# Banded attention and a gated convolution FFN on one core: the planner counts TensorE's changes of array shape, and the work is divided anew

## The chip, the cores and the metric

The kernel runs on one core of one Trainium2 chip. The metric is the device time of one execution in microseconds (us). Five engines work beside each other: TensorE (PE in the profile, its weight loads PEld), VectorE (DVE), ScalarE (ACT), GpSimd (POOL) and SyncE (SP), which here issues nearly all DMAs.

## The reference, cut to what matters

```python
# q, k, v: (8 batches, 8 heads, 576 positions, 64), float32
scores = q @ k.T / 8                      # per batch and head
scores = where(abs(i - j) <= 32, scores, -1e9)
x = softmax(scores) @ v                   # heads joined: (8, 576, 512)
h = maximum(x @ w_in, 0)                  # w_in: 512 x 1024
conv = sum(conv_w[t] * h shifted by t - 1 along the sequence for t in 0, 1, 2)
out = (h * sigmoid(conv)) @ w_out         # w_out: 1024 x 512, out float32
```

## The kernel before, in words

**Attention.** The work of a batch is split by pairs of heads. `cast_qk` and `cast_q_turned` (POOL) make bfloat16 copies of q and k; `tr_mm` transposes them on TensorE into PSUM and `tr_copy` copies them out in two parts, one by ACT and one by DVE, cut at row `CUT` (`CUTH` for the first two batches) of nine. For the batches in `TURNED` a DMA transposes q. Because only a band of 32 positions to each side is needed, scores are computed for a 64-wide query tile against a 128-wide key window. `score` is a matmul with a contraction of 64, so it uses one half of TensorE's rows, and heads of a pair go to the two halves: `sch_mm`, `scl_mm` and `sc_mm` are the row-halves matmuls. ACT takes the exponential, DVE multiplies by the 0/1 band mask. `av_mm` and `avc_mm` multiply by v, with 64 output partitions each: these are the column-halves matmuls. A column of ones beside v gives the sums; DVE divides (`sum_rec`, `av_norm`, `avc_norm`). `castv` (POOL) makes the bfloat16 v, `shift_v` (keys `voc`; POOL, or DVE for batches below `VP`) a copy shifted by 64 rows. The result x is transposed on TensorE (`xt_mm`, first two batches) or by a DMA (`xt_dma`).

**FFN.** The 4608 rows of all batches are cut into 12 chunks of 384 (`c`), and d_ff into 8 blocks of 128 (`m`): 96 conv blocks. `ph_mm` computes a block of h (4 matmuls of some 385 columns), `relu` (ACT) writes it to hT with weight 0.5. The convolution of a block goes one of three ways (`conv_by`): on TensorE (`pc_mm`, 3 matmuls with diagonal weights made by `make_diag`), on ACT and DVE (`conv_acc`: one scaled copy by ACT into PSUM, two multiply-adds by DVE), or on POOL (`conv_pool`, five instructions). `tanh` (ACT) and `gate` (DVE) finish it, `py_mm` multiplies by w_out (8 matmuls of 512 columns for 128 rows), `y_copy` and `y_store` write out. Chunks 0 and 1 are worked in two halves of 192 columns. All FFN and transpose matmuls use the whole array.

**Order.** Each piece of work is entered with `add`: engine, a wished time `want`, a duration, what it depends on and which PSUM banks or buffers it takes and gives back. `Planner.run` is a list scheduler that runs when the program is built: it plays the durations through, picks for each engine among the pieces that could start soonest the one with the earliest `want`, and the pieces are emitted in that fixed order on every engine. Its durations therefore decide the order, not the time on the chip. Where the plan leaves TensorE idle in its first 30 us, `fill` puts in dummy matmuls. Wished times come from constants: `chunk_at(c)` is `S2 + (c - 2) * PC`, batches are placed ahead of their chunks (`want_of_b`), loads ahead of batches (`LEAD`, `LD`).

Of the kernel before, what the change touches and what calls it, by code (L numbers as in the profile page):

```python
# [16 lines left out]
class Op:  # L17
# [3 lines left out]
    def __init__(self, eng, want, dur, lat, fn, deps, takes, gives, dma, early, ring, shared):  # L21
        self.eng, self.want, self.dur, self.lat, self.fn, self.early = eng, want, dur, lat, fn, early
        self.ring, self.shared = ring, shared
        self.deps, self.takes, self.gives, self.dma = deps, takes, gives, dma


class Planner:

# [7 lines left out]
    def add(self, key, eng, want, dur, fn, deps=(), lat=None, takes=(), gives=(), dma=None,  # L36
            early=0.0, ring="SP", shared=False):
        if lat is None:
            lat = {"ACT": 0.16, "DVE": 0.14, "POOL": 0.08}.get(eng, 0.12)
        assert key not in self.ops, key  # L40
        self.ops[key] = Op(eng, want, dur, lat, fn, deps, takes, gives, dma, early, ring,
                           shared or eng == "POOL")

    def run(self, fill, until):
# [16 lines left out]
        order = []  # L61

# [31 lines left out]
        while done < len(ops):  # L94
            best = None
            for e, now in engines.items():
# [8 lines left out]
                if not starts:  # L105
# [22 lines left out]
            engines[e] = start + op.dur  # L128
            end = start + op.dur + op.lat
# [31 lines left out]
def kernel(  # L161
# [27 lines left out]
    BH = 2  # L189
# [118 lines left out]
    QK, V96, V128, WQ = 1.75, 0.9, 1.1, 1.7  # L308
# [277 lines left out]
    def ph_mm(c, m, part, ps):  # L586
        x0, x1 = cols_of(c, part)
        for kc in range(KC):
            x_ = xT_pp[c // 3 % 2][:, x0 // S, kc, x0 % S:x0 % S + min(x1 - x0, S - x0 % S)]
            if x0 < S < x1:  # L590
# [3 lines left out]
                pf[ps[0]][:, 0:x1 - x0], w_in_sb[:, kc, m * 128:(m + 1) * 128], x_,  # L594
# [3 lines left out]
    def relu(c, m, part, ps):  # L598
        kind = c % 3
# [3 lines left out]
        from_ = pf[ps[0]][:, 0:n]  # L603
        if kind == 1 and part is None:
            base = hT[:, m, 0:HW + 1]
            to = bass.AP(base.tensor, base.offset, [list(base.ap[0]), [HW + 3, 2], [1, HW + 1]])
            from_ = from_.rearrange("p (i x) -> p i x", i=2)
        elif kind == 1:
            to = hT[:, m, (HW + 3) * part:(HW + 3) * part + HW + 1]
        else:  # L610
            o0 = (1 if kind == 0 else 0) + x0 - cols_of(c, None)[0]
            to = hT[:, m, o0:o0 + n]
        if relu_by(c, m) == "ACT":
            scalar.activation(to, from_, AF.Relu, bias=0.0, scale=0.5)
        else:
            vector.tensor_scalar(
                out=to, in0=from_, scalar1=0.5, scalar2=0.0, op0=ALU.mult, op1=ALU.max
            )

    def taps(c, m, part, kk):  # L620
        kind = c % 3
        step = HW + (2 if kind == 1 else 0)
        base = hT_pp[kind][:, m, kk:kk + HW]
        return bass.AP(
            base.tensor, base.offset + step * (part or 0),
            [list(base.ap[0]), [step, 2 if part is None else 1], [1, HW]],
        )

    def pc_mm(c, m, part, ps):
        n = CH if part is None else HW  # L630
        for kk in range(3):
            tensor.matmul(
                pf[ps[0]][:, 0:n], diag_w[:, kk, m, :], taps(c, m, part, kk),
                start=(kk == 0), stop=(kk == 2),
            )

    def halves(t_):
        return t_[:, 0:CH].rearrange("p (i x) -> p i x", x=HW)

    def conv_pool(c, m, step, a, b):  # L640

        a, b = halves(ca_pp[a]), halves(cb_pp[b])
        if step in (0, 1, 3):
            kk = (step + 1) // 2
            pool.tensor_scalar(
                out=b if step else a, in0=taps(c, m, None, kk), scalar1=conv_w_sb[:, kk, m:m + 1],
                scalar2=None, op0=ALU.mult,
# [4 lines left out]
    def conv_acc(c, m, kk, ps):  # L652

        to, w_ = halves(pf[ps[0]]), conv_w_sb[:, kk, m:m + 1]
        if kk == 0:
            scalar.activation(to, taps(c, m, None, kk), AF.Copy, bias=0.0, scale=w_)
        else:
            vector.scalar_tensor_tensor(
                out=to, in0=taps(c, m, None, kk), scalar=w_, in1=to, op0=ALU.mult, op1=ALU.add
            )  # L660

    def tanh(c, m, part, ps, from_=None):
        n = CH if part is None else HW
        from_ = pf[ps[0]] if from_ is None else from_
        scalar.activation(pf[ps[0]][:, 0:n], from_[:, 0:n], AF.Tanh, bias=0.0, scale=1.0)

    def gate(c, m, part, ps):
        n = CH if part is None else HW
        o0 = HW * (part or 0)
        vector.scalar_tensor_tensor(  # L670
            out=gT_pp[c % 3][:, m, o0:o0 + n].rearrange("p (i x) -> p i x", x=HW),
            in0=pf[ps[0]][:, 0:n].rearrange("p (i x) -> p i x", x=HW), scalar=1.0,
            in1=taps(c, m, part, 1), op0=ALU.add, op1=ALU.mult,
        )
# [38 lines left out]
    TURNED = (4, 6, 7)  # L713
    XT_N = 2
    DTX = 1.22
    XQ_AT = 0.0
    QW = 1.6
    RELU_DVE = {}
    VP = 2
# [6 lines left out]
    MO, ME = 7.0, 9.0  # L726
    NACT = 3
    LD = 1.7
    PC = 14.2
    S2 = 55.0  # L730
# [12 lines left out]
    DIAG_T = 18.0  # L743
# [28 lines left out]
    for m in range(MB):  # L772
        for kk in range(3):
            engine = "DVE" if kk in DIAG_DVE else "ACT"
# [6 lines left out]
    def qk_loads(b, i):  # L781
# [4 lines left out]
        for y in range(2):  # L786
# [4 lines left out]
            else:  # L791
                got.append((("load", b, y, i), QK, lambda b=b, y=y, i=i: load_qk(b, y, i), after[y]))
# [56 lines left out]
    for b in range(B):  # L849
# [41 lines left out]
        if b < BH:  # L891
            sch = lambda bb: [("sch", bb, f, x, zs) for f in range(2) for x in range(NPH)
                              for zs in HALF_PAIRS[f]] if bb >= 0 else []
            for f in range(2):
# [17 lines left out]
                for i in range(NPH):  # L912
                    for zs in HALF_PAIRS[f]:
# [3 lines left out]
                        add(sk, "PE", ts, 2 * n * 0.021,  # L917
# [9 lines left out]
        for i in range(NPH if b >= BH else 0):  # L927
# [25 lines left out]
            add(lk, "PE", ts, 4 * 0.021, lambda ps, gi=gi: scl_mm(gi, ps), turned + before,  # L953
# [4 lines left out]
            for z in range(2):  # L958
# [3 lines left out]
                add(sk, "PE", ts, 16 * 0.021, lambda ps, g=g: sc_mm(g, ps),  # L962
# [22 lines left out]
        for c in range(NBLK):  # L985
            xdeps = [("ph", (b // 2 - 2) * 3 + z, m, part) for z in range(3) for m in range(MB)
                     for part in (None, 0, 1)]
            if cmajor:
                tx = HALF_AT[b][c > 1] + 4.0 + 0.9 * (c - 2 * (c > 1))
                ak = ("avc", b, c)  # L990
                add(ak, "PE", tx, 16 * 0.026, lambda ps, b=b, c=c: avc_mm(b, c, ps),
# [42 lines left out]
    def relu_by(c, m):  # L1034
        return "DVE" if m in RELU_DVE.get(c, ()) else "ACT"

# [12 lines left out]
    for c in range(NCH):  # L1049
        ps_ = parts.get(c, (None,))  # L1050
        for m in range(MB):
            for part in ps_:
                n = cols_of(c, part)[1] - cols_of(c, part)[0]
                w = CH if part is None else HW
                if c < 2:
                    t = FF_AT[c + part] + FF_STEP[c + part] * m + 0.6 * c * (1 - part)
                else:
                    t = chunk_at(c) + m * PC / (MB + 0.5)
                gap = (3.4 if c == NCH - 1 else 2.4) if part is None else 1.0
                hk, ck = ("ph", c, m, part), ("pc", c, m, part)  # L1060
                add(hk, "PE", t, KC * (n / 2400.0 + 0.003),
                    lambda ps, c=c, m=m, part=part: ph_mm(c, m, part, ps),
# [111 lines left out]
```

## Time and profile before

| | |
|---|---|
| median of 3 runs | 223.59 us (221.87, 223.59, 224.38) |
| profiled execution | 222.25 us, of which the span from first to last instruction is 220.4 us |
| TensorE clock granted | 1.000 |
| PE / DVE / ACT / POOL busy | 208.4 / 181.8 / 187.7 / 169.9 us |
| DMA | 48.28 MB, 219 GB/s over the span |

Busy time of an engine is the union of its instructions' times; idle time inside it is read from the rows' brackets, which name what ended it. The time outside the span, 1.85 us, is taken as it is. Nearly every instruction carries the number of one helper line (L251), so groups are told apart by the tiles they write and read, `out<-in`: `pf` is PSUM.

### The profile page before, as it was taken

To read this page: it belongs to the slowest core of one execution; us is meant where nothing else is said; L and a number is where in the kernel's file an instruction comes from. 1 tells how busy PE (TensorE), PEld (TensorE's weight loads), DVE (VectorE), ACT (ScalarE), POOL (GpSimd) and SP (SyncE) were. 2 spreads that over 40 slices of the span, in tenths; PEclk is the share of its full clock that TensorE was granted. 3 is DMA by queue.
4 is the path that set the end of the run, shared out by engine and by line. 5 is a ranking of instruction groups with operands and counts; after the bars stand their busy time and mean duration, and the time that the engine had idled before them with its cause. 6 is when DMAs were issued, how large, how long until landed. Compare 5 with 4: busy or idle time off the path is not lost.

```text
span 220.4 us, 6695 instructions
## 1 busy us (share of the span) xinstructions
PE 208.4 (95%) x2578; PEld 134.5 (61%) x2602; DVE 181.8 (83%) x361; ACT 187.7 (85%) x414; POOL 169.9 (77%) x204
## 2 busy tenths in 40 slices
PE   7898898999999988998999999999999999999993
PEld 7887797877666655554556555555565555545442
DVE  5388698997659999979898979969899989897930
ACT  3998698987797998699998898888999799999941
POOL 4663865787899999999799997789969449999600
PEclk9999999999999999999999999999999999999999
DMA  5999999996999999999999996999964325121123
GB/s 174 259 247 335 315 265 298 362 315 152 332 336 206 229 330 197 236 301 273 238 280 350 235 216 146 227 322 246 277 162 109 89 73 154 48 95 51 48 95 143
DMA packets 81667, 48.28 MB, mean 219 GB/s; under 512 B 64076, under 2 KB 69476, under 8 KB 81636
## 3 DMA queue, kind: packets, MB, share of 16 engines
q1 hardware_dynamic: 81600, 47.85, 85.4%
q8 instruction: 20, 0.33, 0.7%
q14 instruction: 11, 0.09, 0.1%
q10 hardware_dynamic: 36, 0.01, 0.0%
HBM read 32.52 MB, written 9.44 MB: 190 GB/s over the span
## 4 chain that ended last, share of the span: by engine, by line
PE 63%; DMA 11%; POOL 7%; ACT 6%; SPq 6%; DVE 4%; issue 3%; ACTq 0%; POOLq 0%
PE pf L251 63%; SPq L251 6%; DMA qT<-qb 4%; DMA vst<-in_v_dram 4%; POOL vo L251 3%; DMA wst<-in_moe_w_in_dram 3%; ACT pf L251 2%; ACT hT L251 2%; ACT attn L251 1%; POOL ve L251 1%; DVE attn L251 1%; DVE vo L251 1%; POOL w_in_sb L251 1%; ACT y L251 1%; DVE gT L251 1%
## 5 line engine op out<-in xcount | busy, mean ns | idle before, releaser
L251 PE MATMUL pf<-xT,w_in_sb 128*128 128x385 bf16 (+3 forms) x448 | 75.0, 305 | 2.6 <-POOL w_in_sb L251 0.8
L251 PE MATMUL pf<-w_out_sb,gT 128*128 128x512 bf16 (+1 forms) x272 | 66.1, 373 | 1.2
L251 DVE SCALAR_TENSOR_TENSOR gT<-pf,hT 128x384 bf16<-128x384 f32 (+1 forms) x112 | 52.7, 489 | 8.3 <-ACT pf L251 7.9
L251 PEld LDWEIGHTS <-w_in_sb 128*128 128x128 bf16 x448 | 40.5, 98 | 23.5 <-issue 2.0
L251 DVE SCALAR_TENSOR_TENSOR pf<-hT,conv_w_sb,pf 128x384 f32<-128x384 bf16 x86 | 51.6, 609 | 3.7 <-ACT pf L251 3.2
L251 ACT ACTIVATE hT<-pf 128x385 bf16<-128x385 f32 (+3 forms) x112 | 48.3, 462 | 3.7 <-PE pf L251 3.4
L251 ACT ACTIVATE pf<-pf 128x384 f32<-128x384 f32 (+1 forms) x102 | 43.6, 442 | 4.7 <-PE pf L251 3.2
L251 PEld LDWEIGHTS <-gT 128*128 128x128 bf16 x296 | 28.0, 98 | 28.7 <-issue 0.2
L251 ACT ACTIVATE attn<-pf 128x1024 bf16<-128x1024 f32 (+2 forms) x48 | 37.7, 816 | 0.4 <-PE pf L251 0.3
L251 POOL TENSOR_SCALAR vo<-ve 64x520 bf16<-64x520 bf16 x48 | 33.7, 702 | 3.7
L251 DVE TENSOR_TENSOR attn<-attn,mask 128x1152 bf16<-128x1152 bf16 (+2 forms) x32 | 29.3, 925 | 6.6 <-ACT attn L251 6.4
L251 ACT COPY y<-pf 128x512 f32<-128x512 f32 (+1 forms) x36 | 21.1, 585 | 13.0 <-PE pf L251 12.8
L251 POOL TENSOR_SCALAR ve<-vst 128x512 bf16<-128x512 f32 x40 | 26.6, 669 | 6.9 <-DMA vst<-in_v_dram 5.1
L251 PE MATMUL pf<-hT,diag_w 128*128 128x192 bf16 (+1 forms) x177 | 29.8, 283 | 0.2 <-ACT hT L251 0.2
L251 POOL TENSOR_SCALAR qb<-qst 128x512 bf16<-128x512 f32 (+1 forms) x22 | 19.7, 898 | 9.5 <-DMA qst<-in_q_dram 9.2
L251 DVE TENSOR_TENSOR xn<-pf,rec 128x640 bf16<-128x640 f32 (+1 forms) x34 | 26.3, 778 | 0.4
L251 ACT ACTIVATE pf<-hT,conv_w_sb 128x384 f32<-128x384 bf16 x43 | 25.5, 598 | 0.6 <-DVE xn L251 0.2
L251 POOL TENSOR_SCALAR cb<-hT,conv_w_sb 128x384 f32<-128x384 bf16 x20 | 25.1, 1259 | 0.2
L251 POOL TENSOR_SCALAR kb<-kst 128x1152 bf16<-128x1152 f32 x16 | 19.1, 1195 | 3.4 <-DMA kst<-in_k_dram 3.1
L251 POOL TENSOR_TENSOR ca<-ca,cb 128x384 f32<-128x384 f32 x20 | 20.2, 1019 | 0.5
L251 POOL TENSOR_SCALAR ca<-hT,conv_w_sb 128x384 f32<-128x384 bf16 x10 | 12.4, 1246 | 7.8 <-ACT hT L251 7.7
L251 PEld LDWEIGHTS <-diag_w 128*128 128x128 bf16 x177 | 14.6, 97 | 5.9 <-issue 0.6
(48 smaller groups left out, 227.9 us busy)
## 6 DMA issues: line engine op xcount, KB each, us to landing
out_dram<-y SPq DMA_DIRECT2D x35, 256.0 KB, 3.0
kst<-in_k_dram SPq DMA_DIRECT2D x12, 576.0 KB, 6.7
vst<-in_v_dram SPq DMA_DIRECT2D x24, 256.0 KB, 4.4
qst<-in_q_dram SPq DMA_DIRECT2D x6, 576.0 KB, 7.4
vst<-in_v_dram SPq DMA_DIRECT2D x16, 192.0 KB, 5.5
qst<-in_q_dram SPq DMA_DIRECT2D x6, 512.0 KB, 5.0
qst<-in_q_dram SPq DMA_DIRECT2D x8, 288.0 KB, 6.4
kst<-in_k_dram SPq DMA_DIRECT2D x8, 288.0 KB, 6.0
```

The source lines that it names most:

```text
L251: return lambda *args, **kwargs: fixed(do(*args, **kwargs))
```

## The change

The planner gives each piece of TensorE work a mode (0 whole array, 1 row halves, 2 column halves). A piece whose mode differs from that of the piece before starts 0.097 us later in the plan; after a halves piece, other halves pieces count as wished 3 us earlier. Planned durations of the halves matmuls are lowered, those of the first q and k loads raised (`QK0`). Nearly all constants of the order are set anew. In chunks 0 and 1 `relu`, `tanh` and `gate` take two blocks in one instruction (`PAIR_R`, `PAIR_G`; in chunk 10 `tanh` and `gate` only, where neither block is POOL's). Nine of the 24 diagonal weights are made by DVE. `shift_v` of batch 2 goes to DVE, half of batch 0's to POOL. `CUT` goes from 4 to 5 and `CUTH` from 3 to 2. One load of w_out goes ahead of the first loads of batch 1. POOL has the same blocks as before, but for m = 2 in the place of m = 0 in chunk 8. A block that stands in both lists is POOL's: the lists take 53 blocks off TensorE before and 57 after.

```diff
+    MODES = {"sch": 1, "scl": 1, "sc": 1, "av": 2, "avc": 2}
+    DRAIN = 0.097
...
+        def gain(op):
+            if op.eng != "PE" or not mode or not op.mode:
+                return 0.0
+            return same if op.mode == mode else other
...
-                    key=lambda k: (ops[k].want, number[k]),
+                    key=lambda k: (ops[k].want - gain(ops[k]), number[k]),
                 )
+                if e == "PE" and ops[key].mode != mode:
+                    starts[key] = max(starts[key], now + self.DRAIN)
...
+            if e == "PE":
+                mode = op.mode
...
-    QK, V96, V128, WQ = 1.75, 0.9, 1.1, 1.7
+    QK, V96, V128, WQ = 1.75, 0.9, 1.1, 1.75
+    QK0 = (((1.75, 2.6), (2.0, 1.85)), ((1.85, 1.85), (1.85, 1.85)))
...
-    CUT = 4
+    CUT = 5
-    W1, W2, W3 = 0, 0, 2
-    HALF_AT = ((4.0, 16.0), (24.0, 30.0))
-    FF_AT = (13.0, 24.0, 38.0)
-    FF_STEP = (1.2, 1.6, 1.2)
-    PY_AT = 4.0
-    LEAD = 18.0
-    VOC0 = ("DVE", "DVE")
-    DIAG_DVE = ()
+    W1, W2, W3 = 0, 1, 2
+    HALF_AT = ((4.0, 18.0), (24.0, 30.0))
+    FF_AT = (15.0, 24.0, 32.0)
+    FF_STEP = (1.2, 1.2, 0.8)
+    PY_AT = 0.0
+    LEAD = 6.0
+    VOC0 = ("POOL", "DVE")
+    DIAG_DVE = (0, 1, 2)
-    CUTH = 3
+    CUTH = 2
-    DTX = 1.22
-    XQ_AT = 0.0
+    DTX = 2.0
+    XQ_AT = -1.0
-    VP = 2
+    VP = 3
-    MO, ME = 7.0, 9.0
+    MO, ME = 7.0, 8.0
-    LD = 1.7
-    PC = 14.2
-    S2 = 55.0
+    LD = 1.0
+    PC = 11.0
+    S2 = 54.0
...
-            engine = "DVE" if kk in DIAG_DVE else "ACT"
+            engine = "DVE" if m in DIAG_DVE else "ACT"
...
-                        add(sk, "PE", ts, 2 * n * 0.021,
+                        add(sk, "PE", ts, 2 * n * 0.015 + 0.008,
-                    add(ak, "PE", ta, 20 * 0.024, lambda ps, g=g: av_mm(g, ps),
+                    add(ak, "PE", ta, 20 * 0.0165, lambda ps, g=g: av_mm(g, ps),
...
-    POOL_LAG = 8.0
-    ON_POOL = {2: (0,), 3: (), 4: (0,), 5: (0,), 6: (), 7: (0,), 8: (0,), 9: (0, 2), 10: (0, 2), 11: (0,)}
-    ON_DVE_2 = (1, 3, 4, 6)
-    ON_DVE_3 = (1, 3, 5, 6)
-    ON_DVE_4 = (1, 2, 3, 5, 6)
-    ON_DVE_5 = (1, 3, 5, 6)
-    ON_DVE_6 = (1, 3, 5, 6)
-    ON_DVE_7 = (1, 3, 4, 6)
-    ON_DVE_8 = (1, 3, 5, 6)
-    ON_DVE_9 = (1, 3, 4, 5, 6)
-    ON_DVE_10 = (1, 3, 4, 5, 6)
-    ON_DVE_11 = (1, 2, 4, 5)
+    POOL_LAG = 5.0
...
+    ON_DVE_2 = (0, 3, 5, 6)
+    ON_DVE_3 = (1, 2, 3, 5, 7)
+    ON_DVE_4 = (2, 3, 6, 7)
+    ON_DVE_5 = (0, 2, 5, 6, 7)
+    ON_DVE_6 = (0, 2, 4, 5, 6, 7)
+    ON_DVE_7 = (1, 2, 6, 7)
+    ON_DVE_8 = (0, 1, 3, 4, 5, 7)
+    ON_DVE_9 = (1, 3, 4, 5, 6, 7)
+    ON_DVE_10 = (1, 3, 4, 5, 6)
+    ON_DVE_11 = (0, 1, 2, 4, 5)
...
+    PAIR_R = (0, 1)
+    PAIR_G = (0, 1, 10)
...
-    plan.run(fill, 30.0)
+    SAME, OTHER = 3.0, 3.0
+    plan.run(fill, 30.0, SAME, OTHER)
```

More of the change, by code (lines that the diff above doesn't have):

```diff
@@ L952 @@
             lk = ("scl", gi)
[L953 removed]
+            add(lk, "PE", ts, 4 * 0.015 + 0.008, lambda ps, gi=gi: scl_mm(gi, ps), turned + before,
                 lat=PL, takes=[("p", 2)])
@@ L1032, in conv_by, with groups_of, gates, gates_of @@
         return "POOL" if m in ON_POOL.get(c, ()) else "DVE" if m in ON_DVE.get(c, ()) else "PE"
-    def relu_by(c, m):
-        return "DVE" if m in RELU_DVE.get(c, ()) else "ACT"
+    PAIR_R = (0, 1)
+    PAIR_G = (0, 1, 10)
+    def groups_of(c, conv):
+        got = []
+        for m in range(0, MB, 2):
+            if c in (PAIR_G if conv else PAIR_R) and not (
+                    conv and "POOL" in (conv_by(c, m), conv_by(c, m + 1))):
+                got.append((m, m + 1))
+            else:
+                got += [(m,), (m + 1,)]
+        return got
+    by_relu = {(c, m): ms for c in range(NCH) for ms in groups_of(c, False) for m in ms}
+    by_gate = {(c, m): ms for c in range(NCH) for ms in groups_of(c, True) for m in ms}
+    def gates(c):
+        return [("gate", c, m, p) for m in range(MB) for p in (None, 0, 1)]
+    def gates_of(c, m):
+        ms = by_gate.get((c, m), (m,))
+        return [("gate", c, ms[0], p) for p in (None, 0, 1)]
+    def relu_key(c, m, part):
+        return "relu", c, by_relu[c, m][0], part
     def xt_need(c, part):
```

261 lines of the change are left out of this document (153 added, 108 removed).

## The prediction

> **What bounds the kernel now.** I read the page's busy times first, then a table by stretches, then TensorE's timeline in the middle of the run.
>
> ```profile
> PE 208.4 (95%) x2578; PEld 134.5 (61%) x2602; DVE 181.8 (83%) x361; ACT 187.7 (85%) x414; POOL 169.9 (77%) x204
> ```
>
> The stretches (columns: PE, PEld, DVE, ACT, POOL busy, TensorE clock, DMA share, GB/s) are the start, the stretch of chunks 0 and 1 in half-size matmuls, the long middle with attention and FFN mixed, and the FFN-only end:
>
> ```profile
> 0.00:23.00 23.00, 19.29 (x343) 17.73 (x344) 14.05 (x39) 17.20 (x40) 12.78 (x20) 1.00 0.91 259
> 23.00:50.00 27.00, 25.76 (x431) 22.68 (x430) 23.90 (x57) 23.47 (x70) 18.97 (x24) 1.00 1.07 305
> 50.00:180.00 130.00, 126.63 (x1608) 74.56 (x1627) 114.79 (x211) 115.50 (x234) 110.79 (x137) 1.00 1.00 235
> 180.00:210.00 30.00, 29.64 (x174) 15.74 (x172) 27.30 (x53) 28.65 (x66) 27.38 (x25) 1.00 0.23 74
> ```
>
> From 23 to 210 us TensorE stands idle only 1.24 + 3.37 + 0.36 = 5.0 us, at full clock. DVE is busy 88% and ACT 89% of the middle, 91% and 96% of the end stretch. So TensorE sets the pace, and the two engines behind it have 4 to 12% in hand. Is that busy time work? The timeline of TensorE (start, length, work):
>
> ```profile
> 125.19 1.48 PE L251 MATMUL pf<-xT,w_in_sb 128*128 128x385 bf16 x8
> 126.59 0.23 PE L251 MATMUL pf<-qT,kT 64*128 64x64 bf16 x4
> 126.76 1.90 PE L251 MATMUL pf<-w_out_sb,gT 128*128 128x512 bf16 x7
> 128.59 0.41 PE L251 MATMUL pf<-qT,kT 64*128 64x64 bf16 x16
> 128.93 0.83 PE L251 MATMUL pf<-xT,w_in_sb 128*128 128x385 bf16 x4
> 129.69 0.41 PE L251 MATMUL pf<-qT,kT 64*128 64x64 bf16 x16
> 130.03 0.66 PE L251 MATMUL pf<-hT,diag_w 128*128 128x384 bf16 x3
> ```
>
> Single rows overlap, so prices are start to start. The last of 4 whole-array matmuls of 385 columns ends about 0.33 us after its start, so each takes (0.83 - 0.33) / 3 = 0.166 us, and 8 give (1.48 - 0.33) / 7 = 0.164. A change into row halves: 128.93 + 4 x 0.164 = 129.59, but the scores start at 129.69, 0.10 late. Out of it: 4 scores hold TensorE 0.17 us and 16 hold it 0.34, so one score is (0.34 - 0.17) / 12 = 0.014 and what is left, 0.17 - 4 x 0.014 = 0.11, is the way out. A change costs about 0.105 us, hidden in "busy". That is what the new term of the planner stands for.
>
> **The start** is set by loads. Up to 23 us TensorE runs dummy matmuls between waits:
>
> ```profile
> 7.72 0.96 DVE L251 COPY qT<-pf 128x768 bf16<-128x768 bf16 x1 [2.86 <-PE pf L251]
> ...
> 11.88 2.35 PE L251 MATMUL pf<-warm 128*128 128x128 bf16 x39
> 20.95 4.21 POOL L251 TENSOR_SCALAR w_in_sb<-wst 128x512 bf16<-128x512 f32 x6 [3.08 <-DMA wst<-in_moe_w_in_dram]
> 22.78 0.68 PE L251 MATMUL pf<-xT,w_in_sb 128*128 128x193 bf16 x6 [0.81 <-POOL w_in_sb L251]
> 25.54 1.43 POOL L251 TENSOR_SCALAR qb<-qst 128x1152 bf16<-128x1152 f32 x1 [0.37 <-DMA qst<-in_q_dram]
> ```
>
> POOL waited 3.08 us for the second quarter of w_in and TensorE for POOL's cast; at 22.78 everything is held by that load. SP issues the same loads in the same order up to it in both programs, so the new kernel is at the same place there.
>
> **The change, part by part.** The instruction orders of the two built programs, compared engine by engine, give the counts; the rows of groups (count | busy us, mean ns | idle before) give the prices.
>
> ```profile
> L251 PE MATMUL pf<-hT,diag_w 128*128 128x384 bf16 x81 | 17.7, 327 | 0.2 <-ACT hT L251 0.2
> L251 ACT ACTIVATE pf<-hT,conv_w_sb 128x384 f32<-128x384 bf16 x43 | 25.5, 598 | 0.6 <-DVE xn L251 0.2
> L251 DVE SCALAR_TENSOR_TENSOR pf<-hT,conv_w_sb,pf 128x384 f32<-128x384 bf16 x86 | 51.6, 609 | 3.7 <-ACT pf L251 3.2
> L251 DVE COPY vo<-ve 64x520 bf16<-64x520 bf16 x16 | 5.8, 364 | 1.7 <-POOL ve L251 1.3
> L251 POOL TENSOR_SCALAR vo<-ve 64x520 bf16<-64x520 bf16 x48 | 33.7, 702 | 3.7
> L251 ACT ACTIVATE pf<-pf 128x192 f32<-128x192 f32 x32 | 10.0, 339 | 1.9 <-PE pf L251 1.8
> L251 ACT ACTIVATE pf<-pf 128x384 f32<-128x384 f32 x70 | 33.6, 489 | 2.8 <-PE pf L251 1.5 <-DVE pf L251 1.1
> L251 ACT ACTIVATE hT<-pf 128x193 bf16<-128x193 f32 x24 | 8.0, 354 | 1.7 <-PE pf L251 1.6
> L251 DVE SCALAR_TENSOR_TENSOR gT<-pf,hT 128x192 bf16<-128x192 f32 x32 | 10.1, 345 | 5.1 <-ACT pf L251 5.0
> L251 DVE SCALAR_TENSOR_TENSOR gT<-pf,hT 128x384 bf16<-128x384 f32 x80 | 42.6, 547 | 3.2 <-ACT pf L251 2.9
> L251 DVE COPY kT<-pf 128x640 bf16<-128x640 bf16 x12 | 9.7, 812 | 0.9 <-PE pf L251 0.8
> L251 DVE COPY kT<-pf 128x768 bf16<-128x768 bf16 x4 | 3.8, 950 | 0.1
> ```
>
> *Conv blocks.* TensorE has 12 such matmuls fewer (81 to 69; four blocks, since the named 60 counts three blocks twice). At 0.164 us each that is 12 x 0.164 = 2.0 us; the row's own 17.7 / 81 = 0.218 would make 2.6. I take 2.0. ACT gets 4 x 0.59 = 2.4, DVE 8 x 0.60 = 4.8 us more, behind TensorE as long as they have room.
>
> *Changes of array shape.* Counted in TensorE's order: 124 before, 111 after; 13 x 0.105 = 1.4 us. From the rows above a change could be as little as 0.09 or as much as 0.12: 1.2 to 1.6.
>
> *Pairs.* In chunks 0 and 1, 32 tanh of 339 ns become 16 of 489: 10.8 - 7.8 = 3.0 us off ACT, about as much again for the relu (354 ns singly), and 32 x 0.345 - 16 x 0.547 = 2.3 us off DVE. TensorE's idle there is 1.24 us in all, so I take 0.5 as gain, between 0 and 1.2.
>
> *Copies and v.* Cut at 5, DVE copies 128 elements fewer in 18 copies: (950 - 812) ns x 18 = 2.5 us off DVE; ACT gets at most as many, 0 to 2. Eight shifted copies of v in batch 2 cost DVE 8 x 0.364 = 2.9 us and free POOL of 8 x 0.702 = 5.6. Behind TensorE: 0. The nine diagonal weights go to DVE ahead of its copy at 7.72, for which it waited 2.86 us: 0.
>
> *Start.* One load of w_out now goes ahead of q and k of batch 1. Behind it on SP's queue stand seven loads of that batch, up to its first v; they come later by one such load, 512 KB at the 305 GB/s of this stretch: 1.7 us. The later ones are not shifted, as the second w_out load stood ahead of them before too. Who waits: POOL's cast at 25.54, then TensorE's transposes. Chunk 0 covers TensorE meanwhile, and the new plan puts 19 dummy matmuls behind the second quarter of w_in, against 9: 10 x 2.35 / 39 = 0.6 us. I take 0.6 as loss; uncovered, 1.7. The 29 dummies more ahead of it fall into the wait for w_in.
>
> *Waits in the middle* are few. Two pieces of the chain of waits, then two of TensorE's waits in its timeline:
>
> ```profile
> 73.08 1.01 POOL vo L251
> ...
> 78.78 8.64 DMA vst<-in_v_dram
> ```
>
> ```profile
> 78.51 0.39 PE L251 MATMUL pf<-qT,kT 64*128 64x64 bf16 x15 [0.58 <-DVE gT L251]
> 105.08 0.23 PE L251 MATMUL pf<-qT,kT 64*128 64x64 bf16 x4 [0.64 <-DMA qT<-qb]
> ```
>
> POOL's relief in batch 2 helps the shifted v (vo) in the chain, at 73 us; the loads behind it (vst) stay; DVE's extra 4.8 + 2.9 - 2.5 = 5.2 us hurts. I take 0, from -2 (most of the 3.37 gone) to +3 (as much again).
>
> *End.* After the last normalisation DVE has 30 multiply-adds instead of 26 and 20 gates of one block and 2 of two instead of 24; ACT has about the same. The chain of waits before runs through ACT there:
>
> ```profile
> 203.47 1.26 ACT hT L251 x3
> 206.11 0.51 ACT y L251
> 209.53 5.40 PE pf L251 x25
> ```
>
> DVE's addition is about 4 x 0.60 - 0.3 = 2 us against the 2.7 it has free in 180 to 210, ACT has 1.35 free. I take +0.5, from 0 to +1.5.
>
> **Sum:** -2.0 - 1.4 - 0.5 + 0.6 + 0 + 0.5 = -2.8 us. The profiled execution took 222.25, so 219.4. It lies 1.3 us below the median of the three runs; adding half of that I forecast **220.0 us**. All bounds together: from -2.6 - 1.6 - 1.2 + 0 - 2 + 0 = -7.4 to -2.0 - 1.2 + 0 + 1.7 + 3 + 1.5 = +3.0.
>
> **Rivals.**
>
> *A: the queues behind TensorE become the bound (slower).* Where DVE was full, TensorE already lost time:
>
> ```profile
> 70.00:80.00 10.00, 9.27 (x126) 5.76 (x127) 9.96 (x18) 9.57 (x20) 9.27 (x13) 1.00 1.11 238
> 80.00:90.00 10.00, 9.24 (x134) 5.51 (x128) 9.96 (x20) 8.22 (x19) 9.40 (x12) 1.00 1.18 254
> ...
> 130.00:140.00 10.00, 9.95 (x103) 5.66 (x97) 9.05 (x17) 8.92 (x19) 8.55 (x14) 1.00 0.82 175
> ```
>
> 0.73 and 0.76 us idle of ten in the first two. If the work added to DVE makes the whole middle so, TensorE idles 13 x 0.75 = 9.7 us where it idled 3.4: +6.3 against the -3.4 of less work, so 222.25 + 2.9 = 225.2, and with the same half shift 225.8. It decides once DVE is busy 99% in most stretches; against it, its middle load only rises from 114.8 to some 118 of 127 us, 93%.
>
> *B: nothing to gain on TensorE (no change).* Its busy time would be padding, and removing 3.4 us of it would lengthen waits by the same: 222.9 with the shift. For it: weight loads are busy only 61%. Against it: 8 matmuls follow each other at 0.164 us without a gap. The Trainium skill says on its first page, Trainium Kernel Development and Optimization (Performance Expectations), that matmul busy time is a bad measure of the distance to the limit, as matmuls are pipelined, and that the busy share of the weight loads is a good one. By that rule TensorE would have room; the trace's start-to-start times disagree, so I give it little beyond what waits could do.
>
> *C: the plan fits the chip better (faster still).* With the hidden changes counted, work queued behind them on DVE and ACT comes when planned, and TensorE's idle in the middle falls from 3.4 to about 1, the start loses nothing: -2.0 - 1.4 - 1.2 - 2.4 = -7.0, 215.9 with the shift. For it: 130 to 140 us has 0.05 us idle with DVE at 9.05. Against it: the 0.64 us wait above is for a DMA, whose length no plan changes.
>
> **How the numbers follow.** My forecast (218 to 222): 0.50. C: 0.16. B: 0.19. A: 0.15. A measurement of this kernel can tell about 1% from no change, 2.2 us: faster below 221.35, slower above 225.8. The forecast lies below 221.35 in some 0.85 of its cases, C always: 0.60 faster. A splits about evenly around 225.8, and bad starts of other cases add a little: 0.11 slower. The rest, 0.29, is within 1%. The range reaches from C's 215.9, a little under, to A's 225.8 rounded down, 215.5 to 225.5.
>
> **What would show it.** Right: TensorE's matmuls on diagonal weights of 384 columns count 69; its busy time falls about 3 us less the dummies; idle from 23 to 210 stays near 5 us; the second quarter of w_in is still cast at about 21 us; DVE in the middle about 93% busy. A shows as DVE at 9.9 of ten in most stretches with TensorE waiting for gT or pf; B as TensorE idle up by 3 us or more with DVE unfilled; C as idle below 3. The forecast is wrong if TensorE's first matmul on w_in comes a microsecond later, or if the last y chain begins more than 8 us before the end.

## The result, and the profile after

The changed kernel takes 225.31 us (median of 20 executions, 223.48 to 227.79), the kernel before on the same chip 222.21 (20 executions); the ratio is 1.0104 [1.0070, 1.0138], with its 95% interval in brackets. It is slower by about 1%, where I forecast 220.0 and faster. Half of the changed kernel's executions have a mean granted clock of 0.992 and lie some 2 us above the other half, the profiled one (227.79 us, span 226.1 us) highest of all, and the ratios here leave out executions over 1.5% above the fastest of their kernel, so they are not the ratios of the medians.

The busy times of the changed kernel, from the page of its profile, and the same stretches as before (PE, PEld, DVE, ACT, POOL busy, TensorE clock, DMA share, GB/s):

```profile
PE 211.3 (93%) x2629; PEld 135.8 (60%) x2629; DVE 190.8 (84%) x364; ACT 184.8 (82%) x375; POOL 167.2 (74%) x200
```

```profile
0.00:23.00 23.00, 20.09 (x369) 18.79 (x369) 16.44 (x44) 14.57 (x31) 14.18 (x23) 1.00 0.96 264
23.00:50.00 27.00, 25.59 (x427) 23.20 (x427) 23.16 (x38) 20.79 (x44) 20.09 (x25) 1.00 1.08 304
50.00:180.00 130.00, 122.87 (x1543) 71.03 (x1540) 114.80 (x213) 111.34 (x219) 104.49 (x128) 0.99 1.00 228
180.00:210.00 30.00, 29.96 (x226) 16.11 (x227) 28.80 (x56) 29.38 (x65) 25.04 (x22) 1.00 0.31 93
```

The end is full, the stretch of chunks 0 and 1 about as before. The loss is in the middle: TensorE idles 130 - 122.87 = 7.1 us where it idled 3.4, although DVE has the same 114.8 us of work there and ACT 4 us less. TensorE's busy time did not fall, as I had said it would, but rose from 208.4 to 211.3 us: 39 more dummies (39 x 0.056 = 2.2 us) and a stretch of half clock shown below (1.5 us) are counted in it, and in the trace of before 24 matmuls are missing (2578 records against 2602 weight loads). The groups show that the work moved as counted:

```profile
L267 PE MATMUL pf<-hT,diag_w 128*128 128x384 bf16 x69 | 14.8, 328 | 0.0
L267 ACT ACTIVATE pf<-hT,conv_w_sb 128x384 f32<-128x384 bf16 x47 | 27.6, 596 | 0.3
L267 DVE SCALAR_TENSOR_TENSOR pf<-hT,conv_w_sb,pf 128x384 f32<-128x384 bf16 x94 | 55.7, 613 | 4.0 <-ACT pf L267 1.8 <-PE pf L267 1.8
L267 PE MATMUL pf<-warm 128*128 128x128 bf16 x228 | 16.7, 231 | 1.1 <-DVE warm L267 1.1
```

What TensorE waits for is new. The view of waits (us in total, times, longest), then three places of TensorE's timeline:

```profile
PE pf L267 <- POOL vo L267: 3.5, 3, 1.9
PE pf L267 <- DMA qT<-qb: 2.0, 1, 2.0
```

```profile
125.62 0.19 PE L267 MATMUL pf<-vo,attn 128*64 128x65 bf16 x1 [1.01 <-POOL vo L267]
...
152.50 0.23 PE L267 MATMUL pf<-qT,kT 64*128 64x64 bf16 x4 [2.03 <-DMA qT<-qb]
...
171.70 0.19 PE L267 MATMUL pf<-vo,attn 128*64 128x65 bf16 x1 [1.95 <-POOL vo L267]
```

None of these three is a wait for DVE or ACT. They are for the shifted copy of v, which POOL makes of a load, and for q transposed by a DMA: TensorE, in its fixed order, reaches attention before its operands are there. Not each is there every time: another profiled execution of the same kernel (`a0_again` below) waits 1.12 us for v near 124 us and 2.27 near 168 us, and nowhere for q. The chain of waits runs through the same places; its pieces around the last one:

```profile
143.45 9.01 DMA qT<-qb
152.50 2.02 PE pf L267 x28
...
158.31 0.72 SPq L267
159.08 5.13 DMA vst<-in_v_dram
...
171.03 0.63 POOL vo L267
171.70 8.89 PE pf L267 x68
```

And the last wait has a tail. In the windows around it, with no matmul in the first, the clock is 0.56 in the second, though TensorE is busy in all of it:

```profile
170.00:171.70 1.70, 0.00 (x0) 0.00 (x0) 0.29 (x1) 1.34 (x4) 1.48 (x3) 1.00 0.55 117
171.70:175.20 3.50, 3.50 (x23) 1.74 (x23) 3.01 (x7) 1.73 (x4) 3.37 (x3) 0.56 0.00 0
```

3.5 us at 0.56 cost 3.5 x 0.44 = 1.5 us more.

### The profile page after: what moved, and what is told of

Same layout as the page of the kernel before. It is cut to its first block, busy times and chain, and to the rows that moved or that the text cites. A ratio compares the mean times of both kernels' runs of the same rounds, so it can differ in the third digit from the quotient of the medians.

```text
span 226.1 us, 6725 instructions
## 1 busy us (share of the span) xinstructions
PE 211.3 (93%) x2629; PEld 135.8 (60%) x2629; DVE 190.8 (84%) x364; ACT 184.8 (82%) x375; POOL 167.2 (74%) x200
## 4 chain that ended last, share of the span: by engine, by line
PE 63%; POOL 11%; DMA 10%; SPq 6%; DVE 4%; ACT 3%; issue 2%; POOLq 0%
PE pf L267 63%; SPq L267 6%; POOL vo L267 4%; DMA qT<-qb 4%; DMA wst<-in_moe_w_in_dram 3%; DMA vst<-in_v_dram 2%; POOL ve L267 2%; ACT attn L267 1%; DVE attn L267 1%; POOL ca L267 1%; POOL cb L267 1%; POOL qb L267 1%; ACT pf L267 1%; POOL w_in_sb L267 1%; DVE vo L267 1%
## 5 line engine op out<-in xcount | busy, mean ns | idle before, releaser
L267 DVE SCALAR_TENSOR_TENSOR pf<-hT,conv_w_sb,pf 128x384 f32<-128x384 bf16 x94 | 55.7, 613 | 4.0 <-ACT pf L267 1.8
L267 DVE SCALAR_TENSOR_TENSOR gT<-pf,hT 128x384 bf16<-128x384 f32 (+1 forms) x94 | 51.0, 554 | 4.0 <-ACT pf L267 3.6
L267 ACT ACTIVATE hT<-pf 128x385 bf16<-128x385 f32 (+2 forms) x96 | 46.0, 505 | 6.5 <-PE pf L267 5.8
L267 ACT ACTIVATE pf<-pf 128x384 f32<-128x384 f32 (+1 forms) x84 | 41.3, 498 | 6.1 <-PE pf L267 4.0
L267 DVE TENSOR_TENSOR attn<-attn,mask 128x1152 bf16<-128x1152 bf16 (+2 forms) x32 | 31.3, 987 | 4.2 <-ACT attn L267 3.9
L267 POOL TENSOR_SCALAR vo<-ve 64x520 bf16<-64x520 bf16 x44 | 29.4, 669 | 3.4
L267 ACT ACTIVATE pf<-hT,conv_w_sb 128x384 f32<-128x384 bf16 x47 | 27.6, 596 | 0.3
L267 POOL TENSOR_SCALAR qb<-qst 128x512 bf16<-128x512 f32 (+1 forms) x22 | 21.0, 956 | 9.0 <-DMA qst<-in_q_dram 7.5
L267 PE MATMUL pf<-hT,diag_w 128*128 128x192 bf16 (+1 forms) x165 | 26.2, 280 | 0.9 <-DVE gT L267 0.9
L267 PEld LDWEIGHTS <-attn 128*64 128x64 bf16 x640 | 12.7, 111 | 11.4 <-issue 8.3
```

The lines of the kernel that those rows point to most:

```text
L267: return lambda *args, **kwargs: fixed(do(*args, **kwargs))
```

## The experiments

Four theories. **S (supply):** v and q arrive late for the new order. **Q (queues):** the four more conv blocks on ACT and DVE hold TensorE up, rival A of the prediction. **P:** the planner's new term gathers halves matmuls badly. **R:** each order drawn anew has small waits of its own, with no one cause. In the expectations of the later runs, three forms of S have letters: **H**, SP's standing at the first stores leaves a hole in the loads; **L**, the late stores hold up the last loads; **T**, the stores' traffic meets the loads. Ratios are to the kernel before on the same chip.

### Parts undone, with the order planned anew

`p1_term_off` (the new term without effect):

```diff
-    DRAIN = 0.097
+    DRAIN = 0.0
...
-    SAME, OTHER = 3.0, 3.0
+    SAME, OTHER = 0.0, 0.0
```

> The new kernel, but the planner does not count the changes of array shape (no delay for a change, no preference for halves matmuls); all else as in the new kernel. Its TensorE order has 114 changes where the new kernel has 111. Theory S (supply: the new order has TensorE reach attention matmuls before POOL's shifted v and the transposed q are there, and it stands still in its fixed order): waits of TensorE between 50 and 180 us stay at 6 us or more, 223 to 226 us. Theory Q (queues: four more conv blocks on ACT and DVE): same as the new kernel, 223 to 226. Theory P (the planner's term gathers halves matmuls so that a late v holds up more): waits fall to 4 us or less, 219 to 222.

Measured: 234.23 us, 1.0472 [1.0389, 1.0555].

`p2_old_blocks` (the lists of DVE's and POOL's conv blocks as before, the rest as changed; two of the ten lists of DVE's):

```diff
-    ON_DVE_2 = (0, 3, 5, 6)
-    ON_DVE_3 = (1, 2, 3, 5, 7)
+    ON_DVE_2 = (1, 3, 4, 6)
+    ON_DVE_3 = (1, 3, 5, 6)
```

> The new kernel with the old division of the conv blocks (43 on ACT and DVE, 10 on POOL, TensorE's 177 diagonal matmuls back). TensorE gets 2.0 us of work back. S: waits between 50 and 180 us stay at 6 us or more, 224 to 227. Q: the added work was the cause, so waits fall back to 3 to 4 us, 220 to 222. P: no help, 225 to 227.

Measured: 231.84 us, 1.0436 [1.0379, 1.0492].

`p3_old_times` (the old values of the constants of time alone):

```diff
-    LEAD = 6.0
+    LEAD = 18.0
...
-    LD = 1.0
-    PC = 11.0
-    S2 = 54.0
+    LD = 1.7
+    PC = 14.2
+    S2 = 55.0
```

(and the old `MO, ME`, `DTX`, `XQ_AT`, `POOL_LAG`)

> The new kernel with the old wished times of the middle (LEAD, LD, PC, S2, MO, ME, DTX, XQ_AT, POOL_LAG as before); new division, new start, pairs and the planner's term stay. S, if the wished times make the supply late: waits between 50 and 180 us at 4 us or less, 219 to 221.5. Q and P: no help, 223 to 226.

Measured: 237.02 us, 1.0709 [1.0640, 1.0779].

`p4_term_alone` (the kernel before, with the new term and the lowered durations only):

> The kernel before with nothing but the planner's term and the lowered durations of halves matmuls: 114 changes instead of 124, so 1.0 us less TensorE work. S and Q: waits about as before, 220 to 222.5. P: waits between 50 and 180 us rise from 3.4 to 6 or more, 223.5 to 226.

Measured: 227.91 us, 1.0246 [1.0179, 1.0312].

All are slower than both kernels, and they do not decide on P. `p1_term_off` speaks against it: without the term the changed kernel loses 9 us more, where P had 219 to 222. `p4_term_alone` speaks for it: TensorE idles 130 - 123.53 = 6.5 us in the middle of its profile, as P had said, and the time is above P's 226. But each draws the order anew, and what TensorE waits for is different each time. With the old blocks it idles 10.7 us in the middle, and the longest sums over the run are

```profile
PE pf L267 <- ACT hT L267: 2.4, 2, 2.0
PE pf L267 <- ACT attn L267: 2.2, 4, 0.9
```

The constants fit each other, and a part undone draws the whole order anew, which costs 2.5 to 7% here. From then on I kept the order of instructions as it is and left out work, or moved single instructions.

### The same order, with work left out

`a0_again` is the changed kernel once more, for comparison.

> The new kernel unchanged, as the base of the next three, which keep its order of instructions exactly and only leave work out. 223.5 to 226 us; with the clock at 1.000 throughout, TensorE idle between 50 and 180 us 5 to 7 us.

Measured: 226.36 us, 1.0089 [1.0031, 1.0148]; TensorE waits for vo 3.6 us again.

`a1_no_stores`, in `y_store`:

```diff
+        if c < 9:
+            return
```

> The new kernel's order without the output stores of chunks 0 to 8 (27 DMAs of 256 KB left out, so most of the output is missing). Stores stand in SP's queue ahead of loads and wait there for ACT's y. S (supply): loads and transposes go out earlier, the waits on shifted v and transposed q shrink, 218 to 221.5 us. Q (the queues of DVE and ACT are full): no change, 223.5 to 226. Theory R (with an order drawn anew the waits are many and small, each on something else): at most 1.5 us gained.

Measured: 219.33 us, 0.9837 [0.9770, 0.9904].

`a2_no_shift`, in `shift_v`:

```diff
+        if b > 2:
+            return
```

> The new kernel's order without the shifted copies of v from batch 3 on (40 instructions of POOL left out; those batches multiply by an older v). S: the waits of the value matmuls on POOL, 3.5 us in the profile of the new kernel, go, and with them the half clock behind the longest: 218.5 to 221.5. Q: no change. R: at most 1.5 us gained, as other waits come in their place.

Measured: 222.75 us, 0.9961 [0.9911, 1.0011].

`a3_no_third_tap`, in the multiply-adds of the conv blocks:

```diff
+        if kk == 2:
+            return
```

> The new kernel's order without the third tap of the 47 conv blocks on ACT and DVE (47 multiply-adds of some 0.6 us left out, 28 us of DVE's 191). Q: DVE was the bound, 218 to 221. S: no change, 223 to 226. R: 1 to 2 us gained.

Measured: 224.87 us, 1.0083 [1.0032, 1.0134].

The middle of `a1_no_stores`, and then of `a3_no_third_tap`:

```profile
50.00:180.00 130.00, 127.53 (x1618) 74.90 (x1635) 123.00 (x229) 119.01 (x237) 107.07 (x131) 1.00 0.85 185
```

```profile
50.00:180.00 130.00, 123.27 (x1557) 71.95 (x1573) 103.91 (x188) 114.20 (x227) 104.71 (x129) 1.00 1.00 233
```

Without the shifted copies of v the ratio falls from 1.0089 to 0.9961, some 2.8 us: v's way to TensorE, by the loads and by POOL's copies, is part of the loss. With 11 us less of DVE's work in the middle TensorE idles 6.7 us, as much as with it (7.1, and 6.3 in `a0_again`): Q falls. Without stores it idles 2.5 us, although DVE is now busy 123 of 130 us: DVE at 95% does not hold TensorE up. So S, and by way of the DMA traffic or of SP's queue, both of which the stores share with the loads.

### Is it the stores, and how?

`b0_no_stores` leaves out the same stores in the kernel before.

> The kernel before, its order kept, without the y stores of chunks 0 to 8 (the first 9 of 12 chunks of the output stay unwritten). The changed kernel without them ran at 219.33 us, 7.0 below itself and 1.6% below the kernel before. S (the changed kernel starves in the middle because its loads and transposes come late behind the stores; the kernel before does so less): before has only 3.4 us of TensorE idle in the middle, so it falls by 2 to 3.5 us, to 219 to 220.5, and TensorE's idle from 50 to 180 us falls to 1.5 to 2.5; without stores the two kernels are then within 1 us of each other. R (stores hurt both alike, and the changed order has its own small waits elsewhere): before falls as far as the changed one did, by 6 to 7 us, to 215.5 to 216.5, and the difference of 3 to 4 us stays.

Measured: 222.43 us, 0.9978 [0.9924, 1.0031]. A miss of both: the kernel before gains nothing. Without stores the changed kernel is the faster one by 0.9837 / 0.9978 = 0.986 (with both intervals, 0.977 to 0.994), 3.1 us of 222. Some 0.9 us of it is waiting: in the middle TensorE idles 130 - 126.68 = 3.3 us in `b0_no_stores`, 2.19 of them at 88 us for DVE's xn, against 130 - 127.53 = 2.5 in `a1_no_stores`. The rest, some 2.2 us, is near the -2.8 of my sum: what was taken off TensorE is worth about what I said where nothing else is in the way.

`a4_late_stores` and `b1_late_stores` keep the order but start each y store two of SP's instructions later:

```diff
+            if key[0] == "ys":
+                late.append([key, 2, self.held[("yc", key[1], key[2], 0), "y"][0]])
+                continue
```

> The changed kernel, order kept, but each y store stands two of SP's instructions later in its queue, so that it waits less on y (SP waits 55.4 us for y on 20 stores in the changed kernel, 49.0 before). S, if the delay is SP standing at stores with loads behind it: SP's waits for y fall below 25 us, the middle's TensorE idle falls from 6 to 7 us to 4 or less, and the time falls by 2 to 3 us, to 223 or 224. S, if the delay is the stores' traffic on the DMA engines and not SP's standing there: no change within 1 us (225.5 to 227). R: no change within 1 us.

> The kernel before with the same shift of each y store by two of SP's instructions. S with SP's standing as the delay: falls by less than the changed kernel does, 0 to 1.5 us, to 221 to 222.5. S with traffic, and R: no change within 1 us.

Measured: 227.29 us, 1.0205 [1.0132, 1.0277], and 223.81, 1.0046 [1.0003, 1.0089]. SP's waits for y did fall, here of the changed kernel and then of `a4_late_stores`:

```profile
SPq L267 <- ACT y L267: 55.4, 20, 8.2
```

```profile
SPq L284 <- ACT y L284: 31.5, 13, 7.5
```

Yet the time did not, and SP only stood elsewhere: its waits for DVE's pf grew from 13.7 to 24.6 us and those for xn from 6.6 to 15.4. So these two runs do not show what standing at the stores costs.

`a5_few_dummies` leaves out the last 19 of the dummy matmuls:

> The changed kernel without its last 19 dummy matmuls, those behind the second quarter of w_in (209 left). S, Q and R say the same of the start: the dummies took TensorE about 1.1 us (19 x 58 ns) in a stretch where it had work, so the time falls by 0.5 to 1.1 us if TensorE's queue sets the end, to 225 to 226, and by nothing if the start is held by the loads of batch 1 behind them. A clock below 1 after 23 us would show that the dummies were needed; then it rises by up to 1.5 us.

Measured: 227.08 us, 1.0168 [1.0098, 1.0238]; no gain. Its profile has two stretches at a clock of 0.55 and 0.58, one behind waits of 1.33 and 0.42 us, the other behind one of 2.12 us. The dummies more at the start are not what costs.

`a6_no_early_stores` leaves out the stores of chunks 0 to 2, `a7_no_late_stores` those of 6 to 8, `a8_stores_by_ACT` starts those of chunks 0 to 8 on ACT's queue:

```diff
-        sync.dma_start(out_rows[r0:r0 + 128, w * x:w * x + w], y_pp[y][:, w * x:w * x + w])
+        queue = scalar if c < 9 else sync
+        queue.dma_start(out_rows[r0:r0 + 128, w * x:w * x + w], y_pp[y][:, w * x:w * x + w])
```

> The changed kernel, order kept, without the y stores of chunks 0 to 2 (these rows of the output stay unwritten). H: most of the 7 us come back, 219.5 to 221.5, the DMA share from 56 to 68 us stays near 1 and the waits for the shifted v near 124 and 168 us shrink below 0.5 us. L: 225 to 226.5, these waits stay. T: about a third, 223.5 to 224.5.

> The changed kernel, order kept, without the y stores of chunks 6 to 8. H: 225 to 226.5, and the wait for the shifted v near 124 us stays. L: 219.5 to 221.5, the wait near 168 us goes. T: about a third, 223.5 to 224.5.

> The changed kernel, order kept, with the y stores of chunks 0 to 8 started from ACT's DMA queue in place of SP's: ACT makes y itself, so nothing waits at these stores and SP is free for loads. The traffic is the same. H and L by standing in SP's queue: 219.5 to 222. T: 225 to 227. In every theory ACT pays for 27 DMA starts; if one holds ACT as long as it holds SP (0.36 us at least) that is 10 us of ACT, and the gain could be eaten: then ACT is near 95% in the middle and TensorE waits for hT or pf from ACT.

Measured: 222.48 us, 1.0036 [0.9995, 1.0077]; 225.34, 1.0129 [1.0051, 1.0207]; 225.53, 1.0154 [1.0099, 1.0209].

The stores of the late chunks do not matter. Without those of the first three the ratio is 1.0036 in place of 1.0104, so they make more than half of the loss by these two figures, and the wait near 124 us goes with them. SP's timeline shows what they do first in its queue, in the changed kernel and then in `a6_no_early_stores`:

```profile
52.97 0.42 SPq L267 DMA_DIRECT2D qst<-in_q_dram  x1
59.95 0.37 SPq L267 DMA_DIRECT2D out_dram<-y  x1
60.41 0.39 SPq L267 DMA_DIRECT2D kst<-in_k_dram  x1
61.53 0.36 SPq L267 DMA_DIRECT2D out_dram<-y  x1
61.99 0.39 SPq L267 DMA_DIRECT2D vst<-in_v_dram  x1
64.73 0.35 SPq L267 DMA_DIRECT2D out_dram<-y  x1
65.19 0.38 SPq L267 DMA_DIRECT2D vst<-in_v_dram  x1
```

```profile
53.43 0.77 SPq L267 DMA_DIRECT2D kst<-in_k_dram  x1
54.29 1.53 SPq L267 DMA_DIRECT2D vst<-in_v_dram  x2
```

For 6.6 us SP stands at the first y store, and one k load and two v loads of batch 3 wait behind it, until 65.19 instead of 54.3. (In the kernel before SP stands at such a store there too, but 2.9 us.) The DMA engines move less there, here the kernel before and the changed one in the window of 56 to 68 us:

```profile
56.00:68.00 12.00, 11.84 (x151) 7.42 (x153) 7.78 (x14) 10.15 (x20) 11.05 (x12) 1.00 1.01 318
```

```profile
56.00:68.00 12.00, 11.35 (x179) 7.30 (x177) 11.66 (x23) 9.52 (x16) 3.65 (x4) 1.00 0.78 242
```

Share 0.78 and 242 GB/s against 1.01 and 318 are 0.9 MB less in these 12 us. That this hole makes the wait at 124 us is not shown, and little speaks for it: the last v load of batch 3 starts at 70.5 us with the early stores and at 70.7 without. Near the wait, the two runs differ in a transposing DMA of xn ahead of the v loads of batch 5, first the changed kernel, then `a6_no_early_stores`:

```profile
106.55 3.73 SPq L267 DMA_TRANSPOSE xT<-xn  x1
110.38 2.33 SPq L267 DMA_DIRECT2D vst<-in_v_dram  x3
```

```profile
105.67 1.26 SPq L267 DMA_TRANSPOSE xT<-xn  x1
107.02 2.80 SPq L267 DMA_DIRECT2D vst<-in_v_dram  x3
```

It holds SP 2.5 us longer, and POOL's last copy of that v ends at 125.6 in place of 122.7. Of the runs that keep or nearly keep this order and make these copies, each in which this DMA held SP 3.1 us or more has the wait, and none in which it held SP 2.7 us or less; those without it are `a1_no_stores`, `a6_no_early_stores`, `a8_stores_by_ACT` and `a10`. But `a6_no_early_stores` keeps another wait, near 168 us, as the changed kernel and the other runs so far in this order do, but for `a1_no_stores` and, without the copies, `a2_no_shift`:

```profile
168.27 0.19 PE L267 MATMUL pf<-vo,attn 128*64 128x65 bf16 x1 [2.27 <-POOL vo L267]
```

`a8_stores_by_ACT` has the same wait, and a new one of 1.57 us for xT at 99 us; the one near 124 us is gone, in part since TensorE comes there 0.8 us later. With ACT's queue SP does not stand at the stores, but nothing is gained. The Trainium skill says so on DMA: Bandwidth & Descriptors (Issuing engines are not separate DMA queues): DMAs started by different engines run on the same 16 DMA engines, and only the time to start them is saved. The run's 225.5 us against 225.3 fits that, but does not show it, as ACT pays for 27 starts.

`b2_more_stores` writes the stores of chunks 1 to 3 of the kernel before twice:

> The kernel before with the y stores of chunks 1 to 3 written twice (9 more stores of 256 KB, the same data to the same place). T: at some 240 GB/s the added 2.4 MB take 9.8 us of DMA time in the middle; the kernel before is then starved as the changed one is, 226 to 230. H: the added stores stand where the loads of batches 2 to 4 wait, 225 to 228. If the kernel before has slack in its supply: within 1 us of 222.5.

Measured: 246.64 us, 1.1095 [1.1019, 1.1171], far beyond every theory, and not for the traffic alone. SP waits at the second store until the first to the same place has landed:

```profile
SPq L251 <- DMA out_dram<-y: 33.3, 9, 5.3
```

33 us of standing in SP's queue, with loads behind it, became 25 us of time, part of it as half clock (0.951 in the mean). It says how little room the supply has in the kernel before; it does not part traffic from standing.

### The last wait

With the changed order SP is held long by one transposing DMA of q of the last batch (4.5 us in `a4_late_stores`, 5.7 to 6.8 in the other runs that keep or nearly keep this order). Here the changed kernel, and below it the kernel before:

```profile
149.01 0.65 SPq L267 DMA_DIRECT2D vst<-in_v_dram  x1
149.77 6.41 SPq L267 DMA_TRANSPOSE qT<-qb  x1
...
158.31 3.11 SPq L267 DMA_DIRECT2D vst<-in_v_dram  x3
161.53 2.55 SPq L267 DMA_TRANSPOSE qT<-qb  x1
164.19 0.51 SPq L267 DMA_DIRECT2D out_dram<-y  x1
165.11 0.33 SPq L267 DMA_DIRECT2D vst<-in_v_dram  x1
```

```profile
146.32 1.88 SPq L251 DMA_TRANSPOSE qT<-qb  x1
148.26 0.57 SPq L251 DMA_DIRECT2D vst<-in_v_dram  x1
...
157.46 2.54 SPq L251 DMA_TRANSPOSE qT<-qb  x1
160.04 0.58 SPq L251 DMA_DIRECT2D vst<-in_v_dram  x1
```

The last v load starts at 165.11 and TensorE wants that v at 169.6; before, it started at 160.04 and TensorE came to it at 170.8. It is not the only late one: in the chain above the three loads at 158.31 end the wait of POOL, which then casts and copies with hardly a pause from 164.4 to 171.7. `a9_v_ahead` moves only these loads in SP's queue, and `a10_v_ahead_early_by_ACT` has the stores of chunks 0 to 2 on ACT's queue besides:

```diff
+        for x, ahead in ((1, ("xq", 7, 0)), (2, ("ys", 5, 2, 0)), (3, ("ys", 5, 2, 0)),
+                         (4, ("xq", 7, 1))):
+            keys.remove(("loadv", 7, x))
+            keys.insert(keys.index(ahead), ("loadv", 7, x))
```

> The changed kernel; only SP's order is changed, for the last batch: its second v load goes ahead of the first transposing DMA of its q, the third and fourth ahead of the y store and the transposing DMA of xn behind it, and the fifth ahead of its second transposing DMA of q. The order in SP's queue as the cause: the wait of TensorE for the shifted v near 168 us falls from 2.1 to 2.5 us to below 0.7, the granted clock has no stretch at 0.56 behind it, and the time falls by 2 to 3.5 us, to 222 to 224; the wait near 124 us stays at 1.1 to 1.3 us. If the DMA engines' traffic sets when v arrives, whatever the order: the loads are issued earlier and land later after it, the wait stays above 1.5 us, and the time is 225 to 227. A risk of both: the transposing DMA is later by the 0.6 us of a load, and TensorE waits for q as much longer near 150 us.

> As a9, and the y stores of chunks 0 to 2 are started from ACT's DMA queue, so that SP does not stand at them with the loads of batches 2 and 3 behind it. If hole and order are the causes and add up: 219 to 221, TensorE's idle from 50 to 180 us at 3 us or less, below the kernel before by 0.5 to 1.5%. If a cause is missing: 222 to 225. ACT pays for 9 DMA starts, 3 to 4 us of its time between 55 and 85 us.

Measured: 224.70 us, 1.0101 [1.0041, 1.0161]; 222.89, 1.0023 [0.9977, 1.0068].

In `a9_v_ahead` the wait near 168 us is gone: order in SP's queue was its cause. But the time stayed, because the risk named there came true at four times its size. With two v loads ahead of it, the first transposing DMA of q took 10.4 us to land, where the longest in the changed kernel took 9.0, and TensorE, which came to it 1.5 us sooner, at 158.1 in place of 159.6, stood 2.27 us for it; the half clock followed here. From the chain of waits:

```profile
149.99 10.39 DMA qT<-qb
160.43 18.69 PE pf L272 x199
```

With the first stores off SP's queue as well (`a10`), the k load and the two v loads that stood behind them start from 53.4 us on, as in `a6_no_early_stores`, though up to 68 us no more bytes are moved than in the changed kernel (273 GB/s in the mean in both). SP is then 0.8 us ahead at the transposing DMA, v is not late there and q by 0.65 us at most, the clock stays at 1.00, and TensorE idles 3.2 us in the middle, less than half:

```profile
50.00:180.00 130.00, 126.79 (x1599) 73.33 (x1598) 121.04 (x223) 116.65 (x231) 104.81 (x129) 1.00 0.98 232
```

The loss of 1% is gone, with all work done and only the queues of the DMAs changed: what feeds attention by SP's queue was its cause. But the forecast gain is not reached. One part is a new wait of 1.37 us for xT at 99 us, which in this order only the two runs with stores from ACT's queue have; there ACT starts two stores, at 92.7 and 93.5, beside the DMA for that xT, started at 92.9. By this wait TensorE also comes later to the v near 124 us, so that not all of that wait's end is gain. No version with the full computation beat the kernel before.

## Why the prediction was wrong, point by point

*The work taken off TensorE* (-2.0 and -1.4): right. 69 matmuls on diagonal weights as counted, and start to start a change of shape costs 0.093 to 0.096 us into halves and 0.112 to 0.123 out of them in the trace after, inside my 0.09 to 0.12 but for the last. Where the supply does not interfere the two kernels are 3.1 us apart, some 2.2 of them in work. That also speaks against rival B: the time removed was work. B's sign did come, TensorE's idle up from 5.0 to 8.6 us between 23 and 210 us with DVE unfilled (88% of the middle), but from the waits below and not from padding. The Trainium skill's rule behind it (Trainium Kernel Development and Optimization, Performance Expectations), that the weight loads' busy share tells the distance to the limit, would, by an estimate from the 60% above, have left 40% of room here; the runs without stores show none to speak of.

*Pairs* (-0.5): not seen; TensorE idles 1.41 us from 23 to 50 us where it idled 1.24.

*Start* (+0.6): about right in the rows, somewhat more in sum. The second quarter of w_in is cast 0.46 us later and TensorE's first matmul on it starts at 23.23 in place of 22.78:

```profile
21.41 4.66 POOL L267 TENSOR_SCALAR w_in_sb<-wst 128x512 bf16<-128x512 f32 x6 [2.31 <-DMA wst<-in_moe_w_in_dram]
23.23 0.67 PE L267 MATMUL pf<-xT,w_in_sb 128*128 128x193 bf16 x6 [0.79 <-POOL w_in_sb L267]
```

My alarm, a microsecond, did not ring, and the loss came elsewhere.

*Waits in the middle* ("I take 0, from -2 to +3"): this is the step that failed. The term was put at 0, at +3 at worst, and measured +5.3, with 1.5 of half clock behind it that no term had. Counted by matmul starts, where a wait is the distance to the next start beyond the usual one (so that the modelled tail of 0.2 us of a matmul is not taken for work), gaps of over 0.12 us sum to 8.3 us from 50 to 180 us, against 3.0 before, and 2.8 from 23 to 50 us against 1.8. With the half clock the profiled execution adds up: -3.4 of work, +0.45 at the start, +0.56 for ten dummies, +1.0, +5.3 and +1.5 make +5.4; the spans differ by 5.7.

I had bounded the waits by POOL's relief and DVE's load, and had looked at the DMA waits of before as given ("whose length no plan changes"). But the plan does set how long ahead of its use a load starts. The diff has it: `LEAD` from 18 to 6 and `LD` from 1.7 to 1.0, so that the ninth load of a batch is wished for at `want` + 2 instead of `want` - 4.4. In the planner's own order the last v load of batches 2 to 7 starts so long before the first matmul on that v:

| batch | 2 | 3 | 4 | 5 | 6 | 7 |
|---|---|---|---|---|---|---|
| before, us | 11.4 | 10.8 | 9.6 | 13.3 | 18.3 | 11.9 |
| after, us | 7.3 | 9.8 | 7.8 | 10.1 | 12.4 | 7.6 |

and from SP's start of the last load to the matmul that waited for it the trace has 171.70 - 165.11 = 6.6 us, and 125.62 - 115.21 = 10.4 for batch 5, of which POOL's queue is a part: in both places the last of its copies of that v waited for the work ahead of it on POOL and not for the load. The leads were cut to the length of that chain, in a stretch where the DMA share stood at 1.00 in the very rows that I quoted. That the shorter leads are the reason the stores hurt only the changed kernel fits all these numbers, but was not shown alone: `p3_old_times`, which has the old leads, draws the order anew. Shown is the late supply itself: v loads moved ahead in SP's queue end the wait near 168 us (`a9_v_ahead`), and with the first stores off that queue too the loss is gone (`a10`).

*Rival A* had the sign, the price (225.8) and the wrong engines: not DVE, whose relief changed nothing, but what feeds attention. That its price lies 0.5 us from the measured 225.31 is luck. DVE was not at 9.9 of ten, as it should have been. *C* fails by the same waits. *End* (+0.5): TensorE idles 0.04 us from 180 to 210 us, 0.3 less than before; no loss.

## What to carry to other kernels

When a change takes time off the engine that sets the pace, ask how much earlier that engine will want its next operands, and compare for each stream the lead from the start of its load to its use with the length of the chain in between. Where an order is tuned as a whole, undoing one part says little, since the rest no longer fits: keep the order and leave work out, on both kernels, to see what is in the way. And look along the queue that starts the DMAs: a store that waits for its data, or a transposing DMA that holds the queue, delays every load behind it.

## What was not expected of the hardware

A standstill of TensorE of about 2 us is enough for the half clock afterwards, but not each time: 1.95 us idle in the changed kernel was followed by 3.5 us at 0.56, 2.27 in `a8_stores_by_ACT` by 3.6 us at 0.56; 1.88 in `a7_no_late_stores`, 2.19 at 88 us in `b0_no_stores` and the 2.03 us at 152 us above were not. The clock records of the traces show what parts them. A half clock lasts 3.41 us or twice that, and those of one execution start a whole number of 3.41 us apart (in `a5_few_dummies` at 65.72 and 174.95 us, 32 such periods). From 20 us on, at full clock, each period with 1.95 us or more of standstill was followed by the half clock, two of eight with 1.5 to 1.9 us were, and none with less; the 2.03 us fell on two periods, 1.15 and 0.88. The Trainium skill gives an idle window of about 3.4 us for it, free-running (TensorE: Matmul & The Clock Gate, What's actually happening); here less than a whole window was enough, while the length of the half clock agrees.

One transposing DMA of q held SP for 6.41 us in the changed kernel, and for 5.98 without stores; the other five of the changed kernel held it 2.55 to 3.37 us. The twelve of xn held it 1.33 to 3.73 us in the changed kernel and 1.32 to 2.06 in `a1_no_stores` (before: 1.34 to 3.86, in `b0_no_stores` 1.33 to 2.95), so the stores are part of what holds those. What holds the long one of q is open.
